# Loads by a queue model in a spectral filter and MLP kernel: three queues, weights behind x, twelve tiles turned by DMA

## The chip, the cores and the metric

The kernel runs on one core of one Trainium2 chip. A core has five engines with a queue each: PE (matrix multiplications), DVE, ACT and POOL (element-wise work), and SP, which here only starts transfers. DMA engines, 16 of them, move data between the device memory and the core's memory (SBUF). An instruction waits on semaphores, and everything behind it on its engine waits with it. The metric is device time in microseconds, the median of several executions.

## The reference

A row x of 640 numbers, 2048 of them, is normalised and goes through two branches, whose results are added to x.

```python
x = A_x                                   # 1 x 2048 x 640, bf16
xn = _layernorm(x, axis=-1)
# branch A: a filter in the frequency domain, over both axes
X = rfft2(xn);  X = X * (A_w_r + 1j * A_w_i);  a = irfft2(X)
# branch B: a two-layer network, 640 -> 1536 -> 640
h = gelu(xn @ B_w1 + B_b1);  b = h @ B_w2 + B_b2
return x + a + b
```

The filter weights A_w_r and A_w_i are 2048 x 321 each, in bf16: rows of 642 bytes.

## The kernel before, in words

The 2048 rows are 16 tiles of 128, numbered by c: row 16 p + c of x stands on partition p of tile c. Each tile is normalised into the buffer `xn` (statistics L566 and L568, reciprocal root on POOL L572, the normalisation on DVE L590). There are two `xn` buffers, each for a pair of tiles; the normalisation of a pair waits until everything that read the pair but one before it is done.

A normalised tile goes two ways. For branch B it is turned into `xnT`: tiles 0 to 7 by PE (L605) with a copy out of PSUM (L478 and L479), tiles 8 to 15 by a transposing DMA from SP (L595; `BYDMA` names these tiles). For branch A, sums and differences with the mirrored row (L617, L621) are multiplied with the table `gtab`, the first step of the transform along the rows (groups "a", output `XV`).

Branch A then has the steps b (`etab`, along the 640), c (`mtab`, matmuls of 32 x 32), the filter on DVE (multiplications L722, additions and subtractions L726 with the weights `Wf`), d (`ntab`), a transposing DMA of `U` into `XV` (L747, sixteen of them, from SP), e (`getab`, inverse along the 640), butterflies on DVE (L772, L777), and the last step along the rows with `htab`, which accumulates in the same PSUM banks as branch B's second product. Branch B multiplies `xnT` with `W1` in blocks of tiles (`BLOCKS`: 1, 1, 2, 2, 2, 4, 4 tiles), applies gelu on ACT (L655), and multiplies `gT` with `W2`. For eight tiles (`KEEP`) the second product is made early, b2 is added on DVE (L821) and the sum is kept; for the others b2 is copied by ACT (L800). Then a DMA from POOL, which adds as it writes (an accumulate, L823), adds x to that buffer; the last addition on DVE (L832) joins it with PSUM, and SP stores the tile (L835). The buffers of these sums lie where `xnT` and `X` were (`HOME` names the tiles whose sum lies in `xnT`).

All instructions are described to a scheduler (`Sched`). It simulates the engines with fixed costs and latencies, takes the ready operation with the highest priority, and so fixes the order on each engine; then it works out which semaphores each instruction waits for. A dependency (`reads`, `after`, `deps`) becomes a wait on the chip. A `gate` only keeps the operation back in the scheduler's own simulation: it sets the order and leaves no wait on the chip. `alts` and `rate` are such costs; a transfer's time is there its bytes by a rate, all transfers one behind another. PE's order is fixed in this way too: its products for branch B fill the time between the steps of branch A.

Loads all go out from SP (helper L462) in the order of their text: x and W1 in turns, `gtab`, the rest of x, W2, `etab`, `mtab`, b2, `ntab`, `getab`, `htab`, and then 34 loads of filter weights, among which the transposes of tiles 8 to 15 stand. All filter weights are one buffer `B_w`, so the first multiplication waits for all 34 loads.

Of the kernel before, what the change touches and what calls it, by code (L numbers as in the profile page):

```python
# [10 lines left out]
ALU = mybir.AluOpType  # L11
# [141 lines left out]

LAT = {"pe": 0.2, "dve": 0.125, "act": 0.16, "pool": 0.12}


class Sched:
# [6 lines left out]
    def op(self, engs, prio, emit, reads=(), writes=(), after=(), nbytes=0, gate=(), rate=330e3, alts=None, late=0.0):  # L164
        o = Op()
        o.name = writes[0].name if writes else ""
        o.engs, o.prio, o.emit = engs, prio, emit
        o.reads, o.writes, o.after, o.gate = list(reads), list(writes), list(after), list(gate)
        o.nbytes, o.rate, o.late = nbytes, rate, late
        o.alts, o.alt = alts, None  # L170
        o.seq = len(self.ops)
        o.eng, o.done, o.inc, o.count, o.sem = None, False, False, None, None
        o.deps = [w for b in o.reads for w in b.writers] + list(after)
        for b in o.reads:
            b.readers.append(o)
        for b in o.writes:
            b.writers.append(o)
        self.ops.append(o)
        return o
# [14 lines left out]
    def schedule(self):  # L194
        free = {e: 0.75 for e in self.engines}
        dma_free = 0.0
        self.mode = "128"
# [21 lines left out]
        while left:  # L219
# [47 lines left out]
            if o.nbytes:  # L267
                s = max(t + (1.7 if e == "pool" else 1.1), dma_free)
                dma_free = s + o.nbytes / o.rate
                o.end = dma_free + 0.9  # L270
            else:
                o.end = t + dur + LAT[e]
# [98 lines left out]
BYDMA = tuple(range(8, 16))  # L371
# [8 lines left out]
HOME = (KEEP[:max(0, len(KEEP) - 7)] + tuple(c for c in range(15) if c not in KEEP))[:8]  # L380
WLATE = 19.0
XO = ((0, 3, 6, 15, 1, 2), (4,), (), (5, 7, 8, 9, 10, 11, 12, 13, 14))
# [3 lines left out]
def bass_parallel_sum__spectral_gfnet__dense_activation_gelu__prompt_kernel(  # L386
# [21 lines left out]
    with ExitStack() as es:  # L408
# [52 lines left out]
        def load(dst, src, buf, nbytes, after=(), reads=(), rate=360e3, q="sp", issue=0.45, late=0.0):  # L461
            return K.op([(q, 1.5 if q == "pool" else issue)], 400, lambda e, _: e.dma_start(dst, src), reads=reads, writes=[buf], after=after, nbytes=nbytes, rate=rate, late=late)  # L462
# [37 lines left out]
        B_w = Buf("W")  # L500

        def load_x(c, n, q="sp"):
            o = load(view(X, c * D, [[1, n * D]]), xv[:, c:c + n, :].rearrange("p c d -> p (c d)"), B_x[c], n * D * 256, q=q, rate=375e3 if c else 228e3)
            for i in range(1, n):
                B_x[c + i].writers.append(o)
            return o

        def load_w1(j, q="sp"):
            a, b = W1P[j]
            load(view(W1, 128 * a, [[F, 5], [1, 128 * (b - a)]]), w1v[:, :, 128 * a:128 * b], B_w1s[j], 163840 * (b - a), q=q, rate=320e3)  # L510
        load_x(0, 1)
        load_x(1, 1)
        load(ident[:], const["I"], B_id, 32768, rate=150e3)
        load_w1(0)
        load(b1t[:], b1v, B_b1, 3072)
# [4 lines left out]
        load(gtab[:], const["G"], B_g, 524288)  # L520
        for c in range(6, 16, 2):
            load_x(c, 2)
        for h in range(2):
            load(W2[:, 6 * h:6 * h + 6, :], w2v[:, 6 * h:6 * h + 6, :], B_w2, F * D)
        load(etab[:], const["E"], B_e, 204800, rate=340e3)
        load(mtab[:], const["M"], B_m, 65536, rate=200e3)
        load(b2bc[:], bass.AP(tensor=b2v.tensor, offset=b2v.offset, ap=[[0, 128], [1, D]]), B_b2b, 163840)
        load(ntab[:], const["N"], B_n, 49152, rate=200e3)
# [3 lines left out]
        def load_w(wsrc, p0, off, row, n, step):  # L532
            WL.append(load(bass.AP(tensor=Wf, offset=p0 * WP + off, ap=[[2 * WP, 16], [2 * KP, n], [1, 321]]),
                 bass.AP(tensor=wsrc.tensor, offset=wsrc.offset + row * 321, ap=[[128 * 321, 16], [step * 321, n], [1, 321]]),
                 B_w, 16 * 642 * n, after=[wpad], rate=165e3, issue=0.645, late=WLATE))
        for ri, wsrc in enumerate((A_w_r, A_w_i)):
            for pp in range(2):
                for qq in range(2):
                    for lo in range(2):
                        p0 = 64 * qq + 32 * (lo ^ pp)  # L540
                        m1, off = 32 * qq + 16 * lo + 8 * pp, 16 * pp * KP + ri * KP
                        load_w(wsrc, p0, off, m1, 8, 1)
                        if m1:
                            load_w(wsrc, p0 + 1, off, 128 - m1, 8, -1)
                        else:
                            load_w(wsrc, p0 + 1, off, 64, 1, 1)
                            load_w(wsrc, p0 + 1, off + 2 * KP, 127, 7, -1)
        load(getab[:], const["GE"], B_ge, 204800)
        load(htab[:].rearrange("p a b -> p (a b)"), const["H"], B_h, 524288)
# [10 lines left out]
        for c0, n in [(0, 1), (1, 1)] + [(c, 2) for c in range(2, 16, 2)]:  # L560
# [11 lines left out]
            K.op([("pool", 0.65)], pr, lambda e, _, a=a, b=b: e.tensor_tensor(out=rstd[:, a:b], in0=ve[:, a:b], in1=mhalf[:, a:b], op=ALU.pow),  # L572
                 reads=[B_ve, B_mh], writes=[B_r] + B_rs[a:b])

        for pair in range(8):
# [10 lines left out]
            for n in range(2):  # L586
# [7 lines left out]
                if c in BYDMA:  # L594
                    ring_ops.append(K.op([("sp", 1.3)], 500, lambda e, _, c=c, n=n, xnv=xnv: e.dma_start_transpose(xnT[:, c, :, :], xnv(n, 0, [[1, D]])),  # L595
                         reads=[B_xn, xn], writes=[B_xnT[c]], nbytes=163840, rate=200e3))
# [93 lines left out]
        for P in range(4):  # L690
# [28 lines left out]
            for pair, Y, TB, Z in zip(two, Ys, TBs, Zs):  # L719
                pr = PRIO["filt"] - pair / 5  # L720
                for k in range(2):
                    filt_ops.append(K.op([("dve", dve_us(4 * KP, 2))], pr, lambda e, _, k=k, Y=Y, TB=TB, pair=pair: e.tensor_tensor(  # L722
                        out=view(TT, TB.slot * 8 * KP + k * 4 * KP, [[2 * KP, 2], [KP, 2], [1, KP]]), in0=yv(Y, k == 1), in1=wv(pair, k), op=ALU.mult),
                        reads=[Y, B_w, B_wpad], writes=[TB], after=ring_ops))
# [19 lines left out]
            for pair, U, B_u in zip(two, Us, B_us):  # L744
                for qq in range(2):
                    q = 2 * pair + qq
                    v_ops.append(K.op([("sp", 1.3)], 500, lambda e, _, q=q, qq=qq, U=U, uv=uv: e.dma_start_transpose(  # L747
                        XV[:, :, 128 * q:128 * q + 128], uv(U, D * qq, [[1, D]])), reads=[U, B_u], writes=[B_v[q]], nbytes=163840, rate=200e3))
# [11 lines left out]
        for gi, (c0, n) in enumerate(GROUPS):  # L760
# [20 lines left out]
            for i in range(n):  # L781
# [36 lines left out]
                if kept:  # L818
# [5 lines left out]
                     reads=[xb2], writes=[xo], nbytes=327680, rate=218e3)  # L824
                for o0, w in [(0, D)] if c < 15 else [(0, H2), (H2, Q4), (H2 + Q4, Q4)]:
# [10 lines left out]
                                     reads=[os_, B_o], nbytes=w * 256))  # L836

        for cs, op in zip(XO, (WL[-1], v_ops[3], v_ops[7], v_ops[15])):
            for c in cs:
                xo_ops[c].gate.append(op)  # L840
# [32 lines left out]
```

## Time and profile before

| | |
|---|---|
| three executions | 157.33, 158.47, 162.38 us; median 158.47 |
| profiled execution | span 159.1 us, from the first to the last instruction; the store lands within it |
| PE busy | 146.5 us, 1796 matmuls |
| DVE busy | 108.6 us |
| ACT busy | 81.6 us |
| POOL busy | 21.1 us |
| hardware-generated DMA (SP) | 29368 packets, 17.52 MB |
| software-generated DMA (POOL) | 2304 packets, 5.24 MB |
| mean granted TensorE clock | 0.989 |

The profile gives, for each instruction, its start, its duration, and what ended the idle time of its engine before it. A list of waits adds these up by the pair "who waited for whom". The timeline has the instructions of a stretch in order, merged where they follow one another. DMA views give for each group of transfers the number, the size, and the median time from issue to landing; a landing is the moment when all 16 DMA engines have reported. Stretches can be cut out, with each engine's busy time, the granted clock of PE, the share of the DMA engines' time, and the GB/s moved in them.

The kernel's stages in the profiled execution: x, W1 and tables arrive from 2 to 31 us; the normalisation and the "a" groups run to 46; the first "b" group starts at 47.8; c, the filter and d run to 106; the "e" groups begin at 115.5; the last tiles are finished to 157, and the last store lands at 158.7.

### The profile page before, as it was taken

How to read it: one execution, taken by the hardware profiler on the slowest of the kernel's cores; microseconds unless marked ns; L12 is line 12 of the kernel's file. 1: busy time of each engine (PE TensorE's matmuls, PEld its weight loads, DVE VectorE, ACT ScalarE, POOL GpSimd, SP SyncE). 2: the span in 40 equal slices, each digit the busy share in tenths (PEclk: the TensorE clock that was granted, in tenths of full speed). 3: DMA queues.
4: the chain of work that ended last, by engine and by line, in shares of the span. 5: the costliest groups of instructions: out<-in, count | busy, mean ns of one | idle time of the engine just before them, and what ended most of it. 6: DMA issues, size and time to landing. Idle time of an engine off the chain costs nothing.

```text
span 159.1 us, 4234 instructions
## 1 busy us (share of the span) xinstructions
PE 146.5 (92%) x1796; PEld 94.4 (59%) x1796; DVE 108.6 (68%) x238; ACT 81.6 (51%) x151; POOL 21.1 (13%) x33
## 2 busy tenths in 40 slices
PE   7869899999999995299999999999699989999994
PEld 7758799988756462134554544454266645665563
DVE  2748999999942724939749979731069898798222
ACT  3168988899993637145746535755539400130000
POOL 1202110111600230100202024104002100000000
PEclk9999999999999999879999999999999999999999
DMA  3999999996599594040472388598900833302112
GB/s 102 315 355 407 396 388 228 171 123 139 109 209 147 130 199 103 0 87 6 91 156 50 73 136 184 135 170 139 202 0 4 211 119 124 128 0 82 45 61 62
DMA packets 31690, 23.02 MB, mean 145 GB/s; under 512 B 18104, under 2 KB 28472, under 8 KB 31672
## 3 DMA queue, kind: packets, MB, share of 16 engines
q1 hardware_dynamic: 29368, 17.52, 45.0%
q0 software_dynamic: 2304, 5.24, 15.2%
q8 instruction: 14, 0.23, 0.6%
q14 instruction: 4, 0.03, 0.0%
HBM read 13.58 MB, written 2.62 MB: 102 GB/s over the span
## 4 chain that ended last, share of the span: by engine, by line
PE 68%; DMA 10%; SPq 10%; DVE 6%; issue 2%; ACT 1%; POOL 1%; DVEq 0%
PE ps L467 67%; SPq L462 6%; DMA X<-in_A_x_dram 4%; DMA Wf<-in_A_w_i_dram 4%; SPq L747 3%; DMA XV<-U 2%; DVE T L722 2%; PE ps L605 1%; SPq L595 1%; DVE stats L566 1%; ACT XV L478 1%; DVE W L832 1%; POOL rstd L572 1%; DVE Z L726 1%; ACT T L478 0%
## 5 line engine op out<-in xcount | busy, mean ns | idle before, releaser
L467 PE MATMUL ps<-xnT,W 128*128 128x256 bf16 (+2 forms) x420 | 58.7, 292 | 6.5 <-DVE X L821 4.6
L467 PE MATMUL ps<-W,gT 128*128 128x512 bf16 (+3 forms) x396 | 58.3, 295 | 0.5 <-DVE W L832 0.5
L467 PEld LDWEIGHTS ps<-xnT,W 128*128 128x128 bf16 x420 | 35.0, 98 | 22.5 <-DVE X L821 4.9
L467 PEld LDWEIGHTS ps<-W,gT 128*128 128x128 bf16 x396 | 30.1, 98 | 24.6 <-issue 2.5
L655 ACT ACTIVATE gT<-ps,b1col 128x256 bf16<-128x256 f32 (+2 forms) x84 | 38.7, 510 | 9.8 <-PE ps L467 9.2
L566 DVE BATCH_NORM_STATS2 stats<-X 128x6 f32<-128x320 bf16 x32 | 14.5, 474 | 4.2 <-DMA X<-in_A_x_dram 4.2
L478 ACT ACTIVATE Wf<-ps 128x960 bf16<-128x960 f32 (+1 forms) x8 | 6.7, 868 | 19.6 <-PE ps L467 19.6
L722 DVE TENSOR_TENSOR T<-Y,Wf 128x1288 bf16<-128x1288 bf16 x16 | 12.5, 822 | 4.8 <-DMA Wf<-in_A_w_i_dram 4.8
L823 POOL DMA_DIRECT2D X<-in_A_x_dram x8 | 7.7, 964 | 44.8 <-DVE X L821 44.8
L478 ACT ACTIVATE Xb<-ps 128x960 bf16<-128x960 f32 (+1 forms) x7 | 7.9, 1156 | 7.6 <-PE ps L467 7.6
L478 ACT ACTIVATE Y<-ps 128x644 bf16<-128x644 f32 x8 | 5.7, 707 | 11.1 <-PE ps L467 7.8
L479 DVE CAST Wf<-ps 128x960 bf16<-128x960 f32 (+1 forms) x4 | 4.3, 1072 | 10.0 <-PE ps L467 9.9
L823 POOL DMA_DIRECT2D xnT<-in_A_x_dram x8 | 8.0, 1108 | 22.9 <-ACT xnT L800 12.3
L479 DVE CAST Y<-ps 128x644 bf16<-128x644 f32 x8 | 6.6, 826 | 6.4 <-PE ps L467 6.4
L572 POOL TENSOR_TENSOR rstd<-ve,mhalf 128x2 f32<-128x2 f32 (+1 forms) x9 | 6.2, 694 | 34.7 <-DVE ve L570 34.7
L478 ACT ACTIVATE XV<-ps 128x1280 bf16<-128x1280 f32 (+1 forms) x8 | 9.6, 1196 | 2.1 <-PE ps L467 2.1
L832 DVE TENSOR_TENSOR W<-ps,xnT 128x640 bf16<-128x640 f32 x8 | 6.5, 818 | 5.6 <-PE ps L467 5.4
L479 DVE CAST Xb<-ps 128x960 bf16<-128x960 f32 (+1 forms) x5 | 5.5, 1101 | 5.9 <-PE ps L467 5.8
L467 PE MATMUL ps<-getab,XV 32*128 32x160 bf16 (+1 forms) x128 | 7.7, 242 | 1.4 <-DMA XV<-U 1.4
L832 DVE TENSOR_TENSOR W<-ps,X 128x640 bf16<-128x640 f32 (+2 forms) x10 | 6.7, 686 | 3.1 <-PE ps L467 3.1
L621 DVE TENSOR_TENSOR T<-T 128x512 bf16<-128x512 bf16 (+1 forms) x32 | 8.7, 316 | 0.0
L467 PEld LDWEIGHTS ps<-getab,XV 32*128 32x128 bf16 (+1 forms) x128 | 6.4, 146 | 3.4 <-DMA XV<-U 1.9
(47 smaller groups left out, 132.8 us busy)
## 6 DMA issues: line engine op xcount, KB each, us to landing
xnT<-in_A_x_dram POOLq DMA_DIRECT2D x8, 320.0 KB, 5.5
X<-in_A_x_dram POOLq DMA_DIRECT2D x8, 320.0 KB, 3.9
out_dram<-W SPq DMA_DIRECT2D x15, 160.0 KB, 1.7
X<-in_A_x_dram SPq DMA_DIRECT2D x7, 320.0 KB, 9.8
W<-in_B_w_dram SPq DMA_DIRECT2D x2, 960.0 KB, 12.9
Wf<-in_A_w_r_dram SPq DMA_DIRECT2D x15, 80.2 KB, 6.8
Wf<-in_A_w_i_dram SPq DMA_DIRECT2D x15, 80.2 KB, 2.8
W<-in_B_w_dram SPq DMA_DIRECT2D x1, 800.0 KB, 8.6
```

Source lines behind the costliest of these rows:

```text
L462: return K.op([(q, 1.5 if q == "pool" else issue)], 400, lambda e, _: e.dma_start(dst, src), reads=reads, writes=[buf], after=after, nbyte ...
L467: ins = e.matmul(o_, lhsT=lw, rhs=rh, start=st, stop=sp_, skip_group_check=True)
L478: return e.activation(dst(), src(), ACT.Copy, scale=scale)
L479: return e.tensor_copy(dst(), src())
L566: K.op([("dve", 0.393)], pr, lambda e, _, c=c, h=h: e.bn_stats(stats[:, c, 6 * h:6 * h + 6], view(X, c * D + H2 * h, [[1, H2]])), reads=[B ...
L572: K.op([("pool", 0.65)], pr, lambda e, _, a=a, b=b: e.tensor_tensor(out=rstd[:, a:b], in0=ve[:, a:b], in1=mhalf[:, a:b], op=ALU.pow), read ...
L621: ring_ops.append(K.op([("dve", dve_us(4 * w, 2))], pr, lambda e, _, op=op, x1v=x1v, xfv=xfv, o_=o_, o0=o0, o1=o1, w=w: e.tensor_tensor(ou ...
L655: K.op([("act", act_us(128 * nt, 1))], pr + PRIO["gelu"], lambda e, _, c0=c0, nt=nt, fc=fc, hps=hps: e.activation(gT[:, fc, 128 * c0:128 * ...
L722: filt_ops.append(K.op([("dve", dve_us(4 * KP, 2))], pr, lambda e, _, k=k, Y=Y, TB=TB, pair=pair: e.tensor_tensor(out=view(TT, TB.slot * 8 ...
L747: v_ops.append(K.op([("sp", 1.3)], 500, lambda e, _, q=q, qq=qq, U=U, uv=uv: e.dma_start_transpose(XV[:, :, 128 * q:128 * q + 128], uv(U, ...
L823: xo_ops[c] = K.op([("pool", 0.9)], 51 - c / 20, lambda e, _, c=c, xov=xov: e.dma_start(xov(0, D), xv[:, c, :], accum_op=ALU.add), reads=[ ...
L832: K.op([("dve", dve_us(w))], 95, lambda e, _, os_=os_, fps=fps, o0=o0, w=w, xov=xov, base=base: e.tensor_tensor(out=view(W1, OST + os_.slo ...
```

## The change

- **The scheduler's model of transfers.** Bytes by a rate give way to rows: a table has a time for each row size, and each issuing queue is a ring with limited room, so that an issue can be held back in the simulation. The costs of some issues change with it (0.45 to 0.46, two-tile loads 0.64, POOL 1.15).
- **Three queues.** The identity and the first part of W1 go out from ACT ahead of its table load. b1 goes out from POOL. SP keeps x, the rest of W1, `gtab`, `etab`, `mtab`, `ntab`. POOL takes W2 (four loads of three blocks, instead of two of six), b2, `getab` and `htab`, each with a wait for the landing of x's last pair.
- **Filter weights.** They have four buffers, by real or imaginary (`ri`) and by parity of the pair of columns (`pp`). They follow x on SP, except those with `pp` and `ri` both 1, which go out from POOL with the same wait. The lower bound on their time, `late=WLATE`, is gone.
- **Twelve tiles by DMA.** `BYDMA` is 4 to 15. Tiles 4 to 7 have neither PE transposes nor copies. In the order that the scheduler makes, SP has thirteen weight loads (nine real, four imaginary) ahead of the transposes of tiles 4 and 5, four (imaginary) ahead of tiles 6 and 7, two ahead of 8 and 9, three ahead of 10 and 11, two ahead of 12 and 13, and two ahead of 14 and 15. POOL has the first four of its weight loads ahead of the reciprocal root for tiles 6 and 7, three ahead of that for 8 and 9, one and two of W2 ahead of that for 10 and 11, the other two of W2 and b2 ahead of 12 and 13, `getab` and `htab` ahead of 14 and 15.
- **Accumulates.** What were gates are dependencies, so POOL waits on the chip: the first seven for all filter weights and all transposes of tiles, two for the first four transposes into `XV`, two for the first eight, five for all sixteen. Which sums lie in `xnT` (`HOME`) changes with it.
- The reciprocal root has the highest priority on POOL. PE's order is made anew by the scheduler; its matmuls are the same but for the 20 transposes.

```diff
+class Ring:
+    def __init__(self, lead, room):
+        self.lead, self.room = lead, room
+        self.held = []
+
+    def issue_end(self, t, us, n):
+        end = t + us
+        while True:
+            live = [(f, k) for f, k in self.held if f > end]
+            if sum(k for _, k in live) + n <= self.room:
+                return end
+            end = min(f for f, _ in live)
+
+
+ROW_NS = {256: 18, 384: 22, 512: 27, 642: 34, 768: 37, 1024: 47, 1280: 56, 1600: 68, 2560: 103, 4096: 160, "acc": 170}
+TAIL = 0.9
...
+        rings = {"sp": Ring(1.05, 140), "act": Ring(1.05, 140), "pool": Ring(1.7, 200)}
...
             if o.nbytes:
-                s = max(t + (1.7 if e == "pool" else 1.1), dma_free)
-                dma_free = s + o.nbytes / o.rate
-                o.end = dma_free + 0.9
+                n, size = o.rows
+                ring = rings[e]
+                free[e] = ring.issue_end(t, dur, n)
+                dma_free = max(t + ring.lead, free[e] - dur + ring.lead, dma_free) + n * ROW_NS[size] / 1e3
+                ring.held.append((dma_free, n))
+                o.end = dma_free + TAIL
...
-BYDMA = tuple(range(8, 16))
+BYDMA = tuple(range(4, 16))
...
-HOME = (KEEP[:max(0, len(KEEP) - 7)] + tuple(c for c in range(15) if c not in KEEP))[:8]
+HOME = (1, 2, 4, 5, 7, 8, 14, 15)
 WLATE = 19.0
-XO = ((0, 3, 6, 15, 1, 2), (4,), (), (5, 7, 8, 9, 10, 11, 12, 13, 14))
+XO = ((0, 3, 6, 9, 12, 13, 1), (2, 4), (5, 7), (8, 10, 11, 14, 15))
...
+        load(ident[:], const["I"], B_id, (8, 256), q="act", prio=410)
         load_x(0, 1)
         load_x(1, 1)
-        load(ident[:], const["I"], B_id, 32768, rate=150e3)
-        load_w1(0)
-        load(b1t[:], b1v, B_b1, 3072)
+        load_w1(0, q="act")
+        load(b1t[:], b1v, B_b1, (1, 256), q="pool", prio=95)
         load_w1(1)
...
-        for h in range(2):
-            load(W2[:, 6 * h:6 * h + 6, :], w2v[:, 6 * h:6 * h + 6, :], B_w2, F * D)
...
-                 B_w, 16 * 642 * n, after=[wpad], rate=165e3, issue=0.645, late=WLATE))
-        for ri, wsrc in enumerate((A_w_r, A_w_i)):
-            for pp in range(2):
+                 buf, (n, 642), after=[wpad] + WGATE[q], issue=0.645, q=q))
+        WGATE = {"sp": [], "pool": [x_ops[14]]}
+        for pp in range(2):
+            for ri, wsrc in enumerate((A_w_r, A_w_i)):
+                q = "pool" if pp and ri else "sp"
...
-        load(getab[:], const["GE"], B_ge, 204800)
-        load(htab[:].rearrange("p a b -> p (a b)"), const["H"], B_h, 524288)
+        for h in range(4):
+            load(W2[:, 3 * h:3 * h + 3, :], w2v[:, 3 * h:3 * h + 3, :], B_w2, (24, 1280), q="pool", after=[x_ops[14]], prio=90)
+        load(b2bc[:], bass.AP(tensor=b2v.tensor, offset=b2v.offset, ap=[[0, 128], [1, D]]), B_b2b, (8, 1280), q="pool", after=[x_ops[14]], prio=90)
+        load(getab[:], const["GE"], B_ge, (8, 1600), q="pool", after=[x_ops[14]], prio=89)
+        load(htab[:].rearrange("p a b -> p (a b)"), const["H"], B_h, (8, 4096), q="pool", after=[x_ops[14]], prio=89)
...
-                        reads=[Y, B_w, B_wpad], writes=[TB], after=ring_ops))
+                        reads=[Y, B_w[k, pair % 2], B_wpad], writes=[TB], after=ring_ops))
...
-        for cs, op in zip(XO, (WL[-1], v_ops[3], v_ops[7], v_ops[15])):
+        for cs, ops in zip(XO, (WL + list(TD.values()), v_ops[:4], v_ops[:8], v_ops)):
             for c in cs:
-                xo_ops[c].gate.append(op)
+                xo_ops[c].deps += ops
```

## The prediction

> **What bounds the kernel now.** I read the page's 40 slices first, then the list of waits, then PE's order of work in time, then the DMA view of single stretches. PE is busy for 146.5 of 159.1 us, so only PE's idle time, a lower clock, or matmuls taken away can shorten it. From the waits:
>
> ```profile
> DVE T L722 <- DMA Wf<-in_A_w_i_dram: 4.8, 1, 4.8
> ...
> PE ps L467 <- DVE X L821: 4.6, 1, 4.6
> ...
> PE ps L467 <- DMA W<-in_B_w_dram: 1.5, 1, 1.5
> PE ps L467 <- DMA XV<-U: 1.4, 1, 1.4
> ```
>
> The first two are one event. DVE's first filter multiplication (L722) waits for the last load of the filter weights (issued 56.12, landed 61.92); behind it in DVE's queue stands the addition L821 that frees the PSUM banks PE needs. The busy times by stretch show that it costs more than the idle time (columns: length, then busy us of PE, PEld, DVE, ACT, POOL, then clock, DMA share, GB/s):
>
> ```profile
> 61.60:66.60 5.00, 0.48 (x32) 0.19 (x32) 4.60 (x8) 1.69 (x3) 0.00 (x0) 0.97 0.01 1
> 66.60:70.00 3.40, 3.36 (x18) 1.05 (x19) 1.53 (x3) 0.75 (x2) 0.88 (x1) 0.54 0.44 93
> 70.00:80.00 10.00, 10.00 (x172) 5.52 (x172) 8.18 (x13) 6.03 (x11) 0.88 (x1) 1.00 0.23 52
> ```
>
> After the pause the granted clock is 0.54 for 3.4 us: 0.46 x 3.4 = 1.5 us more. The waits of 1.4 and 1.5 us leave it at 1.00.
>
> The second thing to read is how fast loads flow when the queues are full:
>
> ```profile
> DMA  3999999996599594040472388598900833302112
> GB/s 102 315 355 407 396 388 228 171 123 139 109 209 147 130 199 103 0 87 6 91 156 50 73 136 184 135 170 139 202 0 4 211 119 124 128 0 82 45 61 62
> ```
>
> A slice is 4 us. Up to 24 us the DMA engines are full and move about 390 GB/s; in slices 7 to 9 (24 to 36 us) they are just as full and move 228, 171 and 123. That is where the filter weights, with rows of 642 bytes, stand behind one another. The same in 0.15 us slices, 25 to 31 us:
>
> ```profile
> GB/s 329 255 164 172 109 113 149 113 109 109 145 130 134 206 169 215 124 192 177 126 139 133 120 152 111 137 116 171 218 231 193 176 163 171 150 158 176 197 201 289
> ```
>
> **The change, part by part.** Base: the profiled execution, 159.1 us of span. It is 0.6 us above the median shown (158.47; the runs go from 157.33 to 162.38), so 0.6 comes off at the end.
>
> (a) Weights behind x, in four buffers: **-6.1**. They leave SP right after x instead of after W2, b2, getab and htab, and eight go to POOL. Before, 17 of them came after 37.9 us, between transposes and accumulates. After, SP's last two stand before the transposes of tiles 14 and 15 (normalised at 42 now), so they land near 45, and the first multiplication is due at 57.2: 12 us of cover. 4.56 idle + 1.5 clock go. Next in line is the chain from the second c matmul group to the first d group. It needs four multiplications of 0.74 and four additions of 0.4 on DVE, 4.6 us; the new PE order has about 8.5 us of work between them (18 output matmuls 2.5, the 24 etab 1.25, 18 of 0.22, two c groups 0.9). Covered.
>
> (b) Accumulates held: **-1.4**. In 101 to 116 us the trace has accumulates from POOL among the transposes of U:
>
> ```profile
> X<-in_A_x_dram POOLq DMA_DIRECT2D x2, 320.0 KB, 4.1
> xnT<-in_A_x_dram POOLq DMA_DIRECT2D x1, 320.0 KB, 5.6
> XV<-U SPq DMA_TRANSPOSE x4, 3.1
> XV<-gtab SPq DMA_TRANSPOSE x2, 5.9
> ```
>
> Undisturbed ones land 2.45 to 2.5 us after issue, these up to 6.1. The last four (106.97 to 111.69) would issue every 1.27 us and land at 106.97 + 3 x 1.27 + 2.5 = 113.3, before PE ends its filler at 114.1; now it is 115.48. Behind the new waits on POOL stand only other accumulates. The last five wait for all of XV, then need 5 x 0.9 to 1.24 to issue and 3.5 to 6.7 to land: some 13 us after XV. The addition for tile 8, their first reader, comes some 18 us after XV. At no cover the price would be up to 5 us; I take 0.
>
> (c) Tiles 4 to 7 by DMA: **-1.1**: 20 PE transposes, four groups of 0.28 on the chain. Four copies of 0.43 leave DVE too; DVE is behind PE's filler there, so nothing more.
>
> (d) Start: **-0.5**. W1's first part and ident leave from ACT, b1 from POOL: three issues (0.43, 0.43, 0.54) less on SP, so W1's second part leaves 1.5 us earlier. PE waits 1.5 for it. But by 5 us the DMA engines are full, so what can be won is their idle time before: slices 1 and 2 move 102 and 315 where 390 is full, and most of that is the first latency. Bounds 0 and 1.5; 0.5 is nearer to the 0.7 of idle time between 2 and 5 us. *The Trainium skill*, DMA: Bandwidth & Descriptors, Issuing engines are not separate DMA queues, says the same against this part: DMAs of all issuers run on the same engines and only issue time is saved. By that rule alone the term would be 0 to 1.4.
>
> Sum so far: 159.1 - 6.1 - 1.4 - 1.1 - 0.5 = 150.0.
>
> (e) Tiles 4 and 5 late: **+2.1**. Their transposes stand on SP behind 13 weight loads (twelve full ones). PE's first use of them, in order, is the block 60 matmuls after tile 2's: 26.9 us now (the sixth matmul of the first row here).
>
> ```profile
> 26.35 4.31 PE L467 MATMUL ps<-xnT,W 128*128 128x256 bf16 x38
> ```
>
> After, it is due at 26.9 - 1.1 - 0.5 = 25.3. Their landing: x ends at 18.8 now, 18.3 after; etab, mtab and ntab add 1.05 (their landings now: 0.48, 0.23, 0.34 apart); one weight load of 82 kB takes 0.36 us at 228 GB/s, 0.48 at 171: twelve take 5.0; four from POOL, which start with x's landing, 1.7; two transposes and the tail 1.4. 18.3 + 1.05 + 5.0 + 1.7 + 1.4 = 27.4. Lower bound: 0.27 a load (eight rows an engine at 33 ns, the packets' median at 37 to 42 us): 24.9 with 1.1 for POOL's, no wait. Upper: 0.74 (111 GB/s, the slow 0.15 us slices): 32.6. I take the mean of slices 7 and 8 because those are loads behind a full queue, as here.
>
> (f) The next transposes: **+2.3**. Tiles 8 to 11 land while POOL's W2, b2, getab and htab (2.8 MB) share the DMA engines with them. A transpose beside an accumulate landed in 3.9 to 4.2 instead of 2.45: +1.6 each, four are 6.4. Cover: tile 11 landed 39.26 now, PE used it at 43.4: 4.1. There is a second door: normalised rows have two buffers, so DVE's next pair but one (L590) waits for these landings, with 2.0 us to spare now (35.97 against 38.0), and all else on DVE waits behind it. Bounds 0 and 5 (at 3.5 each, as the worst ones, less cover).
>
> 150.0 + 2.1 + 2.3 = 154.4 in the profile's time; less 0.6: **153.8**.
>
> **Rivals.**
>
> *The queues flow as uncrowded ones* (e 0, f 0 to 2.3): 149.4 to 151.7. For it: uncrowded weights land in 2.0 to 2.5. Against: slices 7 to 9.
>
> *POOL becomes the bound.* 15 loads stand among five rstd instructions (L572 now), which the normalisation needs. At 0.9 to 1.0 us an issue, rstd of tiles 6 and 7 is reached at 18.3 + 4 = 22.3, before it is due at 23.4, and later ones keep up. At 1.6 (the longest POOL issue now, at 55.63), tiles 10 and 11 are reached at 36.5 (now 32.7) and 14 and 15 at 46 (now 41.2): 5 us, plus part of the clock loss, in place of (f): 157.5 to 160. The W2 loads have three times the rows of any POOL load in the trace, which speaks for it; beside a busy DVE, at 42.0, two issues took 1.03 and 1.24 against 0.88 alone, which speaks against much more. *The Trainium skill*, SBUF — State Buffer, the warning on the "DVE blocks DMA" trap, has POOL's descriptor writing locked out while DVE runs its two-port modes; the 1.24 agrees with little of it.
>
> *Slower: tiles 4 and 5 far too late.* From 0.74 us a load, sixteen take 11.8, and if the tables before them stretch as htab did (first engine 24.93, last 30.22, some 2 us more than x), they land at 18.3 + 3 + 11.8 + 1.4 = 34.5. That is 7.1 past (e), and a pause of that length brings the low clock, 1.5: 162.4. It decides from a landing at 33.7 on.
>
> *It doesn't do what it says*: the weights still land late, since 34 loads keep their 0.6 us issue and ring room; 158.5. Against: 12 us of cover.
>
> **How the numbers follow.** A measurement of this kernel tells about 2% (3.2 us) from no change: 155.3 to 161.6. Forecast with (e) and (f) of 152 to 156.5: 0.43. Free-flowing queues: 0.18. POOL: 0.21. Far too late: 0.14. Not as said: 0.04. Faster: 0.18 + 0.33 of the forecast's 0.43 = 0.51. Within 2%: 0.10 + 0.21 + 0.04 = 0.35. Slower: 0.14. Range 150.5 to 160.5: a small part of the free-flowing case and the slow one are left out.
>
> **What would show it.** (a): no wait of L722's successor for Wf, clock 1.00 throughout 55 to 75. (b): no PE wait for XV. (c): 20 fewer transposes. (e): a PE wait for the transposes of T into xnT near 25 us, about 2 us; landing of tile 5 near 27.4. (f): waits of PE or DVE for transposes between 36 and 47. First etab matmuls near 49.9 (now 47.8: +0.5 and +2.3, less three matmuls, 0.65, done later). The forecast is wrong if those waits are missing (too slow a guess), or if rstd or tile 4 holds PE for over 5 us.

## The result, and the profile after

The changed kernel is **slower**: median 166.69 us of four runs (164.34 to 169.27) against 158.56 for the kernel before (157.33 to 162.38); ratio 1.042, 95% interval 1.030 to 1.054. The forecast was 153.8 with a range of 150.5 to 160.5. Executions of one kernel fall into a faster and a slower state: the ratios use the faster ones alone, the medians use all, and the profiles of kernels 1 to 4 and 12 below are of slower ones, so of these only stalls and landings are compared. The profiled execution of the changed kernel has a span of 164.0 us (159.1 before) at a mean clock of 0.969. Line numbers below are those of the changed kernel: norm L618, sums for the "a" groups L645 and L649, PE's matmuls L490, transposes of tiles L623, filter L750.

PE's clock, the DMA engines' share and the GB/s, on the page of after (a slice is 4.1 us):

```profile
PEclk9999999599955999999999999999999999999999
DMA  5999999999999869800084519494647562302112
GB/s 150 383 409 395 185 133 154 145 324 265 94 123 268 140 134 233 196 3 6 16 115 87 111 44 98 94 179 82 131 97 167 124 200 96 129 21 80 40 50 74
```

The dip of the clock at 66 us, where DVE had waited for weights, is gone. There are two new places: the eighth slice (29 to 33 us), and the twelfth and thirteenth (45 to 53). The DMA engines stay full until 53 us, where they were full until 36 before. The list of waits of after (us in total, times, longest):

```profile
DVE T L618 <- DMA xnT<-T: 13.8, 3, 7.5
...
PE ps L490 <- DVE T L649: 6.2, 1, 6.2
PE ps L490 <- DMA xnT<-T: 5.3, 1, 5.3
```

All three end with the landing of a tile's transpose. PE in order of time, with its idle time in brackets:

```profile
22.42 1.25 PE L490 MATMUL ps<-xnT,W 128*128 128x256 bf16 x10
28.98 4.47 PE L490 MATMUL ps<-xnT,W 128*128 128x256 bf16 x25 [5.30 <-DMA xnT<-T]
...
48.74 1.25 PE L490 MATMUL ps<-gtab,T 128*128 128x128 bf16 x10 [6.20 <-DVE T L649]
...
59.41 0.96 PE L490 MATMUL ps<-etab,XV 128*128 128x160 bf16 x16
```

The first "etab" group starts at 59.41; in the kernel before:

```profile
47.79 0.97 PE L467 MATMUL ps<-etab,XV 128*128 128x160 bf16 x16
```

The second stop has a longer story, which DVE's order shows:

```profile
39.76 0.88 DVE L649 TENSOR_TENSOR T<-T 128x512 bf16<-128x512 bf16 x3
48.10 0.45 DVE L618 TENSOR_SCALAR T<-X,mv,rstd 128x640 bf16<-128x640 bf16 x1 [7.46 <-DMA xnT<-T]
48.46 0.22 DVE L649 TENSOR_TENSOR T<-T 128x128 bf16<-128x128 bf16 x1
```

PE needs the fourth L649 of tiles 10 and 11, an instruction of 0.22 us. It stands behind the normalisation of tile 12, which waits for its buffer, which tile 9's transpose holds until 48.02. The busy times by stretch (length, busy us of PE, PEld, DVE, ACT, POOL, then clock, DMA share, GB/s) show what each stop costs beyond the idle time:

```profile
29.00:33.40 4.40, 4.40 (x28) 3.28 (x28) 4.31 (x15) 1.88 (x4) 1.72 (x3) 0.63 1.19 142
...
48.70:54.00 5.30, 5.26 (x39) 4.33 (x40) 5.22 (x17) 3.08 (x6) 0.87 (x1) 0.62 1.06 247
...
60.00:70.00 10.00, 10.00 (x154) 5.72 (x153) 5.73 (x7) 6.29 (x9) 3.43 (x4) 1.00 0.91 204
```

The clock of 0.63 and 0.62 behind the stops costs 0.37 x 4.4 = 1.6 and 0.38 x 5.3 = 2.0 us.

**The account.** Up to the first etab group: two stops 5.30 + 6.20 and low clock 1.6 + 2.0 make +15.1; tile 4 would have been used at 22.42 + 1.25 = 23.67 instead of 26.9, so the start and the transposes taken from PE gave -3.2; three first-layer matmuls more are left for later, -0.65. That is +11.2 of the +11.62 measured. From there to the end: 111.3 us before, 104.6 after, -6.7. Together +4.9, the difference of the two spans. This is the account of two executions. By the ratio the change costs 4.2%, between 6 and 7 us: a time is some 1.8 us longer than its span (165.84 and 164.0 here), so the profiled 159.1 of before is a time of about 160.9 (an estimate from these two numbers), longer than three of the four times of before.

### The profile page after: what moved, and what is told of

It reads as the page before. It is cut to its first block, busy times and chain, and to the rows that moved or that the text cites. A ratio compares the mean times of both kernels' runs of the same rounds, so it can differ in the third digit from the quotient of the medians.

```text
span 164.0 us, 4228 instructions
## 1 busy us (share of the span) xinstructions
PE 147.5 (90%) x1776; PEld 95.1 (58%) x1776; DVE 107.9 (66%) x236; ACT 81.7 (50%) x149; POOL 30.9 (19%) x49
## 4 chain that ended last, share of the span: by engine, by line
PE 62%; DMA 19%; DVE 11%; ACT 3%; issue 1%; SPq 1%; POOL 1%; DVEq 0%
PE ps L490 62%; DMA xnT<-T 13%; DVE stats L594 4%; DMA X<-in_A_x_dram 4%; DMA XV<-U 2%; DVE T L649 2%; DVE T L618 2%; DVE T L645 1%; ACT U L501 1%; SPq L485 1%; DVE W L860 1%; ACT XV L501 1%; ACT gT L683 1%; POOL rstd L600 1%; DVE mv L596 1%
## 5 line engine op out<-in xcount | busy, mean ns | idle before, releaser
L490 PE MATMUL ps<-xnT,W 128*128 128x256 bf16 (+2 forms) x420 | 60.1, 298 | 6.0 <-DMA xnT<-T 5.3
L490 PE MATMUL ps<-W,gT 128*128 128x512 bf16 (+3 forms) x396 | 57.9, 295 | 0.5 <-DVE W L860 0.5
L490 PEld LDWEIGHTS ps<-xnT,W 128*128 128x128 bf16 x420 | 36.1, 101 | 23.0 <-issue 7.2
L683 ACT ACTIVATE gT<-ps,b1col 128x256 bf16<-128x256 f32 (+2 forms) x84 | 39.3, 507 | 14.1 <-PE ps L490 13.0
L490 PEld LDWEIGHTS ps<-W,gT 128*128 128x128 bf16 x396 | 30.1, 98 | 24.4 <-issue 2.2
L851 POOL DMA_DIRECT2D xnT<-in_A_x_dram x8 | 6.9, 979 | 55.9 <-DMA XV<-gtab 20.6
L618 DVE TENSOR_SCALAR T<-X,mv,rstd 128x640 bf16<-128x640 bf16 x16 | 6.6, 442 | 14.0 <-DMA xnT<-T 13.8
L750 DVE TENSOR_TENSOR T<-Y,Wf 128x1288 bf16<-128x1288 bf16 x16 | 12.4, 823 | 0.0
L490 PE MATMUL ps<-gtab,T 128*128 128x128 bf16 x80 | 6.3, 231 | 6.2 <-DVE T L649 6.2
L860 DVE TENSOR_TENSOR W<-ps,xnT 128x640 bf16<-128x640 f32 (+2 forms) x10 | 6.8, 688 | 5.8 <-PE ps L490 5.8
L490 PEld LDWEIGHTS ps<-gtab,T 128*128 128x128 bf16 x80 | 5.4, 104 | 6.8 <-DVE T L649 6.5
L649 DVE TENSOR_TENSOR T<-T 128x512 bf16<-128x512 bf16 (+1 forms) x32 | 8.4, 317 | 0.0
```

The lines of the kernel that those rows point to most:

```text
L490: ins = e.matmul(o_, lhsT=lw, rhs=rh, start=st, stop=sp_, skip_group_check=True)
L618: o = K.op([("dve", 0.356)], pr, lambda e, _, c=c, n=n, xnv=xnv: e.tensor_scalar(out=xnv(n, 0, [[1, D]]), in0=view(X, c * D, [[1, D]]), sc ...
L649: ring_ops.append(K.op([("dve", dve_us(4 * w, 2))], pr, lambda e, _, op=op, x1v=x1v, xfv=xfv, o_=o_, o0=o0, o1=o1, w=w: e.tensor_tensor(ou ...
L683: K.op([("act", act_us(128 * nt, 1))], pr + PRIO["gelu"], lambda e, _, c0=c0, nt=nt, fc=fc, hps=hps: e.activation(gT[:, fc, 128 * c0:128 * ...
L851: xo_ops[c] = K.op([("pool", 0.9)], 51 - c / 20, lambda e, _, c=c, xov=xov: e.dma_start(xov(0, D), xv[:, c, :], accum_op=ALU.add), reads=[ ...
L860: K.op([("dve", dve_us(w))], 95, lambda e, _, os_=os_, fps=fps, o0=o0, w=w, xov=xov, base=base: e.tensor_tensor(out=view(W1, OST + os_.slo ...
```

## The experiments

Twelve kernels in two groups. A ratio is to the kernel before on the same chip, with its 95% interval.

| kernel | ratio | span of the profile |
|---|---|---|
| after | 1.042 (1.030 to 1.054) | 164.0 |
| 1 tiles 4 to 7 on PE again | 1.054 (1.043 to 1.066) | 166.8 |
| 2 POOL's loads after tile 11 | 1.015 (0.995 to 1.036) | 161.9 |
| 3 SP's weights behind tile 5 | 0.994 (0.975 to 1.013) | 157.7 |
| 4 weights spread over 128 partitions | 0.985 (0.955 to 1.014) | 156.0 |
| 5 one queue, eight tiles | 0.968 (0.957 to 0.978) | 150.9 |
| 6 before, only accumulates held | 0.987 (0.977 to 0.997) | 153.7 |
| 7 third xn buffer | 1.026 (1.005 to 1.047) | 159.4 |
| 8 W2 from SP, rest of POOL's after tile 11 | 1.009 (0.985 to 1.032) | 156.7 |
| 9 kernel 5, accumulates as gates | 0.986 (0.974 to 0.998) | 153.0 |
| 10 kernel 5, one weight buffer | 0.983 (0.972 to 0.994) | 151.5 |
| 11 kernel 5, twelve tiles | 1.018 (1.007 to 1.029) | 157.6 |
| 12 only POOL's W2 and tables after tile 11 | 1.011 (1.002 to 1.021) | 158.8 |

### Which transfers make the tiles late

**1. Eight tiles by DMA, all else as after.**

```diff
-BYDMA = tuple(range(4, 16))
+BYDMA = tuple(range(8, 16))
```

> The changed kernel with tiles 4 to 7 turned by PE again (BYDMA 8 to 15); the scheduler then puts all 26 weight loads of SP ahead of the transposes of tiles 8 to 15. Theory W (the transposes are late because weight loads are stacked ahead of them on SP): the wait of 5.3 us for tile 5 and the slow clock behind it (1.7) go, 1.1 us of PE transposes comes back; the 26 loads are through by about 34 us, tile 9 lands by 36 instead of 48, DVE's wait of 7.5 goes too; span 149 to 152. Theory P (they are late because POOL's loads take turns with them on the DMA engines, 5120 bytes against 256 a turn): the first wait goes as well, but tile 9 still lands after 40 and DVE waits 3 us or more; span 154 to 158.

Measured: the stop at 24 us is gone, and it helps nothing: all 26 weight loads of SP now stand ahead of tile 8. Tile 8 issues at 28.88 and lands at 44.99, tile 9 at 30.34 and 51.39, while W2 lands between 36 and 49. One stop takes the place of two:

```profile
52.61 2.29 PE L490 MATMUL ps<-xnT,W 128*128 128x512 bf16 x5 [11.97 <-DMA xnT<-T]
```

So the late tiles 8 and 9 do not come from the four transposes added ahead of them. Nor do they only wait for the weights in their own queue: the last of the 26 loads has landed at 35.45, and tile 8 takes 9.5 us more beside W2. The spans, 162.8 to 166.8 in four executions, lie above what either theory said.

**2. POOL's fifteen loads wait for tile 11's transpose.**

```diff
+for o in K.ops:                 # POOL's loads; b1 (prio 95) and the accumulates left out
+    if o.rows and o.engs[0][0] == "pool" and o.prio != 95 and o.rows[1] != "acc":
+        o.deps.append(TD[11])
```

> The changed kernel with all 15 loads of POOL (eight of weights, W2, b2, getab, htab) made to wait for the landing of tile 11's transpose. Theory W: tile 5 still lands at 27 to 29 behind 13 weight loads, PE still waits 4 to 5 us and then runs slow; tile 9 stays late by the weights ahead of it; span 160 to 164, plus what W2 costs by arriving late. Theory P: tile 5 lands by 25.5 (wait under 2 us, clock kept), tiles 8 to 11 land within 5 us of their issue, DVE's waits of 2.8, 3.5 and 7.5 go; span 150 to 153.

Measured: tile 5 lands at 25.18 (28.89 in after), tiles 8 to 11 land 3.4, 2.7, 2.9 and 2.7 us after their issue. Transposes issued between 29 and 32 us, in after and then here (median us to landing):

```profile
xnT<-T SPq DMA_TRANSPOSE x2, 14.6
```

```profile
xnT<-T SPq DMA_TRANSPOSE x2, 3.0
```

The landings are as theory P said, the span (156.8 at best, 150 to 153 expected) is not. The cost moves on: W2 lands only from 53.2 to 61.5, tile 15, issued beside it at 43.81, lands at 57.28, and PE stops for W2:

```profile
61.52 4.65 PE L490 MATMUL ps<-W,gT 128*128 128x512 bf16 x19 [5.37 <-DMA W<-in_B_w_dram]
```

**12. Only W2, b2, getab and htab wait for tile 11; POOL's eight weight loads stay.**

```diff
+for o in K.ops:                 # POOL's W2, b2, getab, htab
+    if o.rows and o.engs[0][0] == "pool" and o.prio in (89, 90):
+        o.deps.append(TD[11])
```

> The kernel after with POOL's eight weight loads left where they are and only its W2, b2, getab and htab held until tile 11 is turned. It tells which of POOL's loads delay which tiles. If weights and W2 each delay the tiles beside them: tile 5 lands near 28.5 as in the kernel after (PE wait 4 to 5.5), tiles 8 and 9 within 6 of their issue, DVE waits 2 to 5 for xnT instead of 13.8, W2 lands after 50 and PE waits 3 to 6 for it, span 161 to 164. If it is the weights that delay all: tile 9 lands over 10 after its issue, DVE waits over 8.

Measured, PE's stops and DVE's waits:

```profile
28.09 5.49 PE L490 MATMUL ps<-xnT,W 128*128 128x256 bf16 x25 [4.35 <-DMA xnT<-T]
54.59 1.80 PE L490 MATMUL ps<-W,gT 128*128 128x512 bf16 x12 [1.81 <-DMA W<-in_B_w_dram]
```

```profile
DVE T L618 <- DMA xnT<-T: 3.7, 2, 1.9
```

The first case, with W2's stop (1.81, 3 to 6 expected) and the span (158.8, 161 to 164 expected) smaller than said. Tile 5 is nearly as late as in after (28.00 against 28.89), tiles 8 and 9 land 6.0 and 3.3 us after their issue instead of 12.9 and 16.3, and DVE waits 3.7 instead of 13.8. This separates the two stops: with POOL's **weights** beside them tiles 4 and 5 are late, with POOL's **W2 and tables** tiles 8 and 9. That POOL's loads are not the whole cause of either, 3 and 4 show.

**3. SP's weights may start only from 19 us of the simulated time,** which puts them behind tile 5's transpose.

```diff
+for o in WL:
+    if o.engs[0][0] == "sp":
+        o.late = 19.0
```

> The changed kernel with SP's weight loads held back to 19 us in the scheduler's simulation, with no wait on the chip: the transposes of tiles 4 and 5 then stand right behind ntab, five weight loads ahead of 6 and 7, two or three ahead of each later pair, twelve after tile 15; POOL is as in the changed kernel. Theory W: tile 5 lands by 22, tile 9 by 37, no wait for either; span 149 to 152, unless the last weights, issued to about 50 us, are late for the filter. Theory P: tile 5 lands by 25 (POOL's weights beside it), but tile 9 still lands after 42 beside W2, and DVE and PE lose 6 to 8 us there; span 156 to 159.

Measured: tile 5 lands at 23.33, and PE does not stop for it, although POOL's weights are where they were. Tile 9, issued at 29.19 beside POOL's W2, still lands 10.0 us later. PE's stops of over 1.2 us after the start:

```profile
39.92 1.25 PE L490 MATMUL ps<-gtab,T 128*128 128x128 bf16 x10 [4.20 <-DVE T L649]
...
46.83 0.81 PE L490 MATMUL ps<-xnT,W 128*128 128x512 bf16 x3 [1.28 <-DMA xnT<-T]
```

The second is for tiles 10 and 11, landed at 46.02 and 46.74. So tiles 4 and 5 need two things to be late, SP's own weights ahead of them and POOL's weights beside them: without the first they land at 23.33, without POOL's loads (2) at 25.18, with both at 28.89. Tiles 8 and 9 stay late beside W2.

**8. W2 and b2 on SP right behind x, the rest of POOL's loads after tile 11, SP's weights as in 3.**

```diff
-load(W2[...], w2v[...], B_w2, (24, 1280), q="pool", after=[x_ops[14]], prio=90)
+load(W2[...], w2v[...], B_w2, (24, 1280))       # ahead of etab; b2 behind ntab
...
+    o.deps.append(TD[11])                       # POOL's weights, getab, htab, as in 2
...
+    o.late = 19.0                               # SP's weights, as in 3
```

> The kernel after (twelve tiles by DMA) with W2 and b2 on SP right behind x, SP's weights behind tile 5's transpose, and POOL's weights, getab and htab issued only once tile 11 is turned. Theory P: no queue has large packets beside tiles 4 to 11, tiles 4 and 5 land at 22 to 24, tiles 8 to 11 within 4 us of their issue, W2 lands before 26, no DVE wait for xnT over 1.5; first etab 45.5 to 47.5, span 150 to 152, time 152 to 154. Rival: the transposes' own rate is the bound (twelve tiles at 1.3 us of SP each and the weights between them): tiles 10 and 11 land after 40, first etab after 50, time 156 to 160.

Measured: W2 lands at 22.9, tiles 8 to 11 land 4.5, 3.7, 3.2 and 2.7 us after issue, the first etab group starts at 45.54: the landings are as expected, though tiles 4 and 5 come at 24.9 and 25.6. The span is not: 156.7. Neither theory said that. PE is never held by a tile, but it has eight idle times of 0.6 to 1.35 us (7.8 together) with six different causes (b1, gtab, the gelu on ACT, DVE's copies, issue, the final addition); kernel 5 has two of 0.5. A milestone in the middle also misled: kernel 8 reaches etab early with more first-layer matmuls still to do (127 against 105 in kernel 5).

**4. The same bytes of weights in rows of 642, each load written to 128 partitions with one row instead of to 16 partitions with eight.** The loads of one and of seven rows become one of eight, and a load reads 128 neighbouring rows instead of 16 groups of eight. The filter then multiplies by other numbers.

```diff
...
-ap=[[2 * WP, 16], [2 * KP, n], [1, 321]]                   # where the rows go in Wf
+ap=[[WP, 128], [1, 321]]
-ap=[[128 * 321, 16], [step * 321, n], [1, 321]]            # where they are read
+ap=[[321, 128], [1, 321]]
```

> The changed kernel with the same number of weight loads, rows of 642 bytes and bytes, but each load writes 128 rows to 128 partitions instead of 8 rows to each of 16 partitions two apart (the weights then stand in other places, so the filter multiplies by other numbers). If the slow stretches (rows of 642 bytes at 60 to 90 ns and more, 33 alone) come from sixteen partitions of one group of 32 being written at once, rows take 33 to 40 ns all through, tile 5 lands near 25 and the wait of 5.3 shrinks to 1 or 2 without loss of clock; span 157 to 160, less if tile 9 also comes early. If they come from the size of the rows or from the number of queues, nothing changes: 163 to 165.

Measured: the 13 weight loads ahead of tile 4 land between 18.65 and 21.72 (after: 20.64 to 24.05). A packet of 642 bytes took 33 ns at 18 to 20 us (median of 814), in after 74 ns (median of 490); in the 2 us before, the median was 33 in both. Tiles 4 and 5 land at 24.60 and 24.87, PE's stop for them falls to 0.6 (released by ACT), tiles 8 and 9 land 7.4 and 6.6 us after their issue, at 34.75 and 35.20, with POOL's W2 still beside them; tiles 10 and 11 still come at 43.15 and 43.68, beside getab and htab, and PE stops 3.31 us for them. The time falls from 1.042 to 0.985 of before with the intervals apart. So a good part of the loss hangs on the form of the weight loads, that of tiles 8 and 9 too. The partitions written and the addresses read changed together here, and which of them counts was not tried apart. *The Trainium skill*, SBUF — State Buffer, Door 1: The DMA port swizzle, has a transfer's rate go by the ports that its partitions reach; sixteen partitions, every second one of 32, reach eight of sixteen by its table. The 74 against 33 ns agrees in direction with that, as far as the partitions are the cause.

**7. A third xn buffer (in U2, which is written much later).**

```diff
-p_xn = Pool(2)
+p_xn = Pool(3)
...
-return view(TT, XN + xn.slot * 2 * D + n * D + o, dims)
+return view(U2, n * D + o, dims) if xn.slot == 2 else view(TT, XN + xn.slot * 2 * D + n * D + o, dims)
```

> The kernel after with three buffers for the normalized pairs instead of two (the third lies in U2, which is written only much later). Theory C (the late tiles cost that much because DVE's next norm needs their buffer back): DVE's wait for xnT falls from 13.8 to under 8, DVE T at the gtab matmuls of PE from 6.2 to under 3, first etab 53 to 57, time 159 to 163. Rival (the tiles' own landing is what PE needs, buffers or not): first etab 58 to 60, PE waits 5 or more for xnT of tiles 8 to 11 in place of the wait for T, time 164 to 168.

Measured: DVE's wait for tiles falls to 7.4, PE's stop for L649 from 6.20 to 0.30, with a stop of 1.21 for a tile itself; the first etab group starts at 52.45. The stop for tile 5 is unchanged (5.4). So the second stop is tile 9 through the buffers; a third buffer takes 4.6 us off the span and does not pay for the queues.

### What the parts are worth without the late tiles

**5. All late loads and weights on SP, eight tiles by DMA:** what is left of the change is four weight buffers, held accumulates, the early start, and the order that the new model of transfers makes.

```diff
-BYDMA = tuple(range(4, 16))
+BYDMA = tuple(range(8, 16))
-q = "pool" if pp and ri else "sp"
+q = "sp"
...                              # W2, b2, getab, htab on SP too; o.late = 19.0 for WL
```

> The kernel after with POOL's 15 late loads and all weights back on SP (W2, the tables, b2, getab and htab behind x, the 32 weights behind them) and only tiles 8 to 15 turned by DMA: what is left of the change is the four weight buffers, the accumulates held by semaphores and the earlier start. Theory P (the loss is POOL's packets among the transposes): the first etab matmul starts between 46.0 and 47.8, no wait of over 1 us for xnT, tiles 8 and 9 land within 6 us of their issue as before, no wait of DVE for Wf, none of PE for XV; from the first etab on the kernel after needed 104.6 us, so the span is 150.6 to 152.4 and the time 152.5 to 154. Theory W (weights ahead of the transposes in SP's own queue do it, whatever POOL does): tiles 8 and 9 land over 8 us after their issue, DVE waits 6 or more, first etab after 53, time 157 to 160.

Measured: as theory P said: etab at 47.30, transposes issued at 29 to 32 us land in 3.2, no wait for Wf or XV, span 150.9, time 152.52. From its page:

```profile
PE 145.7 (97%) x1796; PEld 94.2 (62%) x1796; DVE 110.1 (73%) x238; ACT 80.7 (53%) x151; POOL 21.9 (15%) x34
...
PEclk9999999999999999999999999999999999999999
```

This kernel beats both: 3.2% under before (2.2 to 4.3), and PE has 5.2 us of idle time left.

**6. Before, with only the accumulates held.**

```diff
-xo_ops[c].gate.append(op)       # op: WL[-1], v_ops[3], v_ops[7], v_ops[15]
+xo_ops[c].deps += ops           # ops: WL, v_ops[:4], v_ops[:8], v_ops
```

> The kernel before with only its accumulates held by semaphores (the first group behind the landing of all 32 weights, the others behind the landing of XV 0 to 3, 0 to 7 or 0 to 15) instead of by the simulated order. Theory of the prediction: the PE wait of 1.4 for XV near 115 goes and the transposes of U land within 3 us of their issue; in the first 62 us the weights no longer share the DMA engines with four accumulates, so the last weight lands up to 4 us before 61.9 and DVE's wait for Wf (4.8) shrinks by as much: the span is 157.7 if only the XV wait goes and 153.5 if the weights come 4 us earlier; time 155 to 159. Rival: holding the accumulates makes the final adds wait for them at the end, span 160 to 163.

Measured: the span is 153.7, the upper of the two effects expected. The wait for XV is gone and the last weight lands at 57.21 instead of 61.92, since no accumulate stands among the weights. DVE's first multiplication, in this kernel:

```profile
57.29 2.31 DVE L722 TENSOR_TENSOR T<-Y,Wf 128x1288 bf16<-128x1288 bf16 x3 [1.08 <-DMA Wf<-in_A_w_i_dram]
```

Its wait was 4.83 in the profile of before. So one edit removes nearly all of the stall that the prediction's first term gave to the weights' place and buffers. (The loads are 34, where the expectation says 32.) It removes a spread as well: its five executions have spans of 153.2 to 153.8, all at a clock of 1.00; the nine of before on that chip have 154.7 to 160.4, one of them at 1.00. The gain by the ratio is 1.3%, some 2 us, less than the two profiles show.

**9. Kernel 5 with the accumulates as gates; 10. kernel 5 with one weight buffer.**

```diff
-xo_ops[c].deps += ops                                       # 9; XO and HOME as before
+xo_ops[c].gate.append(op)
-B_w = {(ri, pp): Buf(...) for ri in range(2) for pp in range(2)}   # 10
+B_w = {(ri, pp): one for ri in range(2) for pp in range(2)}
```

> The one-queue kernel (weights in four buffers, early start, eight tiles by DMA) with the accumulates put back to the simulated order that the kernel before has, so that four weight buffers and the start are left. Theory S (the four buffers carry most of the gain, as the prediction's first term said): DVE still does not wait for Wf, PE waits 1.4 or so for XV before the first getab matmul, span 152 to 153.5. Theory H (holding the accumulates carries it, because it is the accumulates beside the weights that made the last weights late): weights land late again, DVE or PE waits 2 or more near 60, span 155 to 159.

> The one-queue kernel with one buffer name for all weights instead of four, so that the first filter waits for all 32 loads; accumulates stay held. In the one-queue kernel the last weight landed at 56.9 and the first filter multiply started at 56.0. Theory H: the buffers are worth no more than 0 to 1.2 once the accumulates are held: span 150.9 to 152.3. Theory S: a stall of 4 to 6 at the first filter, slower clock behind it, span 155 to 158.

Measured: kernel 9 has a span of 153.0 with a PE stop of 1.41 for XV and one of 1.50 near 61 us; DVE waits 1.51 for the second half of the weights, which land to 59.42 among accumulates. Kernel 10: 151.5, DVE waits 1.04 for Wf. The spans are as theory S for 9 and theory H for 10 had them (but 9 does wait for Wf), and together they say that neither is right alone: either the buffers or the held accumulates remove most of the stall at 62 us, and the second of them adds 0.6 (buffers) or 2.1 (held accumulates, with the XV wait), by one profile each.

**11. Kernel 5 with twelve tiles by DMA.**

```diff
-BYDMA = tuple(range(8, 16))
+BYDMA = tuple(range(4, 16))
```

> The one-queue kernel with twelve tiles turned by DMA instead of eight: W2, tables, getab and htab stand ahead of tile 4 in SP's queue, the weights between the later tiles. Theory Q (a transpose waits for what stands ahead of it in its own queue): getab and htab landed at 25.6 and 28.7 in the one-queue kernel, so tile 4 and 5 land at 27 to 30, PE waits 4 to 6 for them as in the kernel after, span 155 to 158. Rival (it is only POOL's packets that delay tiles 4 and 5): they land before 25, four transposes fewer on PE (1.1), span 149.8 to 151.

Measured: tiles 4 and 5 land at 26.67 and 27.38, theory Q's mechanism, and the span, 157.6, lies in its range, but not for its reason: no stop of PE is for a tile. PE's idle times of over 0.4:

```profile
14.09 0.73 PE L490 MATMUL ps<-gtab,T 128*128 128x128 bf16 x10 [0.97 <-DMA gtab<-c_G]
...
30.32 2.01 PE L490 MATMUL ps<-xnT,W 128*128 128x256 bf16 x15 [0.60 <-ACT gT L683]
34.58 2.01 PE L490 MATMUL ps<-xnT,W 128*128 128x256 bf16 x15 [0.60 <-ACT gT L683]
39.28 2.14 PE L490 MATMUL ps<-xnT,W 128*128 128x256 bf16 x18 [1.04 <-ACT gT L683]
61.02 0.50 PE L490 MATMUL ps<-Xb,mtab 32*32 32x322 bf16 x32 [2.30 <-DVE Xb L502]
...
101.17 0.52 PE L490 MATMUL ps<-Z,ntab 32*32 32x320 bf16 x32 [0.78 <-ACT U L501]
136.09 3.43 PE L490 MATMUL ps<-W,gT 128*128 128x512 bf16 x24 [1.35 <-DVE W L860]
```

PE has 20 transposes less to do and 6.9 us more idle time than in kernel 5. The largest, 2.30, is a DVE copy behind a multiplication that waits 2.60 for the weights now placed behind the tiles. The others are small and have no common cause: PE's order was made anew for each kernel, and ACT's gelu paces it at 30 to 40 us. Why twelve tiles cost so much there stays open; that they bring nothing with one queue or with three (1 against after, intervals overlapping) is measured.

## Why the prediction was wrong, step by step

**(a) and (b), -6.1 and -1.4: right for the profiled execution, too large for others, and wrong in what does it.** From the first etab group on, the profile became 6.7 us shorter, where the two terms, less 0.65 of matmuls pushed behind it, give 6.85 by the prediction's own count. No multiplication waits for Wf, no matmul for XV, the clock is 1.00 there. But the stall was read from one long execution: 159.1 of span is a time of about 160.9, 2.4 above the median of 158.47 and not 0.6. Nine of the 29 other executions of before whose clock is on record had a mean clock of 1.00, at spans of 153.4 to 155.4: the 1.5 us of low clock in the term was not in them. By the ratios kernel 5, which has (a), (b) and (d), gains 3.2%, some 5 us, where these terms add up to 8.0. And the terms overlap, as kernels 6, 9 and 10 show: the weights were late because accumulates stood among them. Against the profile of before, holding the accumulates alone gives -5.4 of span, new buffers with the early start and the new order -6.1. Priced apart, each term would have been off.

**(c) and (d), -1.6: the size stays open.** Tile 4's first use came 3.2 us earlier: W1's second part landed at 7.60 instead of 9.93, tile 2's x at 8.42 instead of 10.72. With (c) at its 1.1 that would leave 2.1 for the start, past the bound of 1.5. But kernel 6 has the loads of before in their old order, and there W1's second part landed at 7.98, and PE came to the row that the prediction shows at 26.35 earlier:

```profile
25.39 4.31 PE L467 MATMUL ps<-xnT,W 128*128 128x256 bf16 x38
```

So some 0.96 of the 2.1 lies between two executions and not in the change, and the rest is within the bounds. *The Trainium skill*, DMA: Bandwidth & Descriptors, Issuing engines are not separate DMA queues, has only issue time saved, by which the prediction had up to 1.4. No run here decides against that. Term (c) by itself did not show as a gain in any kernel.

**(e), +2.1: right place, too small.** The stop was 5.30 and 1.6 of low clock, 6.9. Of the difference, 1.6 is the earlier due time (23.67 instead of 25.3), 1.5 the landing (28.89 instead of 27.4), 1.6 the clock, which was priced for (a) but not for a stop that grows past it. Tile 5 lands at 25.18 without POOL's loads, so they cost it 3.7, where the step had 1.7 for four of them; 0.9 of the 3.7 goes with W2 and the tables (28.00 in 12). The lower bound in this step adds up to about 25.1 and not 24.9; nothing hangs on it.

**(f), +2.3: the step that failed, by size.** The mechanism was named, the door of the two buffers too, and measured it cost 6.2 and 2.0 of clock, 8.2, past the upper bound of 5. The price of 1.6 a tile came from transposes beside an accumulate. Tiles 8 and 9, beside W2 and the tables, landed 12.9 and 16.3 us after their issue; with those loads held (12) 6.0 and 3.3; with them, but the weights spread over 128 partitions (4), 7.4 and 6.6. One row for "beside POOL's queue" was carried over to other transfers: an accumulate in before is 128 packets of 2560 bytes, POOL's W2 and b2 are 416 of 5120. Nor is it a price for each tile: the two weight loads ahead of tile 8 on SP (issued at 27.70 and 28.34) landed 10.9 and 13.2 us after their issue, so the whole of SP's queue was late. How the delay comes about was not separated. *The Trainium skill*, DMA: Bandwidth & Descriptors, Queues, rings and completion order, says that a DMA engine goes round the queues packet by packet. The trace of after agrees in part of the stretch only: at 38 to 40 us 92 of POOL's packets (201 ns, median) and 119 of the transposes' 256 bytes (18 ns) were moved, but at 34 to 36 us 106 and 545, at 40 to 42 us 29 and 827. And POOL has only some 37 packets an engine in W2 and the tables, 7.4 us at 201 ns (an estimate from these rows), which does not account for 16.3.

**The sum.** Of the 9.6 us between the 154.4 of the prediction and the span of 164.0, (f) is 5.9 and (e) 4.8; the start and the transposes gave 1.6 back, and 0.5 is left over. In time the miss is 12.0, 153.8 against 165.84 for the profiled execution: the 1.8 by which a time is longer than its span, and the 0.6 that was taken off, come on top.

**The rivals.** POOL did not become the bound: its load issues took 0.53 to 0.78 us, less than an accumulate (0.85 to 1.56), and the reciprocal roots were not late for them. *The Trainium skill*, SBUF — State Buffer, the "DVE blocks DMA" trap, warns of a lock-out of POOL's descriptor writing beside DVE. In these issue times it did not show. Free-flowing queues are what kernel 5 shows, in one queue. "Tiles 4 and 5 far too late", the case that ended slower, was to decide from a landing at 33.7; tile 5 came at 28.89 and the kernel is slower all the same, by (e) and (f) together, where that case had (e) alone grow.

## What to carry to other kernels

A latency that is read beside one kind of transfer holds for that kind alone: before loads go to a second queue, ask which short transfers with a waiting reader will share the DMA engines with them, and at what packet sizes. A stall that is read from one execution is held against the spread of the others before its whole size is taken off the median. Where a buffer pair couples an engine to a landing, look in that engine's order for small instructions behind the waiting one. Two remedies for one stall are priced together, not added.

## What the chip showed that was not expected

- Loads of 16 groups of eight rows to 16 partitions took 74 ns a row of 642 bytes where loads of 128 neighbouring rows to 128 partitions took 33 ns, in the same stretch of the kernel (18 to 20 us); 2 us earlier the median was 33 in both.
- POOL's queue joins rows: its weights go as packets of 4494 bytes (seven rows), W2 as 5120 bytes.
- Pauses of PE of 3.3 us and more were followed by a lower clock (0.63 and 0.62 in the stretches after 5.30 and 6.20 in after, 0.50 after 3.31 in kernel 4); pauses up to 2.3 us (11) were not.
